# Sinkhorn-sorted attention with top-1 experts: q loaded first, sort operands made earlier

## The chip, the cores and the metric

One NeuronCore of a Trainium2 chip runs the whole program; the other cores are idle. The metric is the device time of one execution in microseconds (us), lower is better. Engine names: PE is TensorE, DVE is VectorE, ACT is ScalarE, POOL is GpSimd, SP is SyncE. PSUM is the memory into which PE writes; the other engines evict results from it to SBUF.

## What is computed

Two stages, one after the other (q, k, v: batch 4, 8 heads, 768 rows, head width 64, float32):

```python
P = sort_net                                   # (4, 8, 8, 8)
for _ in range(5):
    P = np.exp(P - P.max(-1, keepdims=True))
    P = P / (P.sum(-1, keepdims=True) + 1e-09)
    P = P / (P.sum(-2, keepdims=True) + 1e-09)
k_sorted = np.einsum('bhij,bhjcd->bhicd', P, k_b)   # 8 blocks of 96 rows
v_sorted = np.einsum('bhij,bhjcd->bhicd', P, v_b)
attn = softmax(scale * q_b @ k_sorted.T)       # inside each block of 96
x = (attn @ v_sorted), as 3072 rows of 512
e = argmax(x @ w_gate)                         # 8 experts
out = softmax(x @ w_gate)[e] * (relu(x @ w1[e]) @ w2[e])
```

The expert weights are 512 x 1024 and 1024 x 512 for each of 8 experts.

## The kernel before

The work runs batch by batch (four batches of 768 rows). For batch b the kernel guesses one expert from the mean of v (the vote: vote_sum and vote_pick on PE, vote_read on DVE, lines 222 to 245), POOL reads the winner into a register (read_vote) and loads that expert's w1 and w2. All 768 rows of the batch go through that expert; rows of another expert would be done in a loop behind everything (line 704), which is entered only if the count rest_i is over zero.

Order. manual_schedule keeps every engine's instructions in the order in which the code emits them. So the order of the lines is the order in each engine's queue, and an instruction that waits holds all later ones of its engine. All loads of q, k, v and weights are issued by POOL (they convert float32 to bf16 on the way), in one queue; the two small loads and the output go by SP.

Start (lines 129 to 335). POOL issues v, q and k (three parts) of batch 0. PE spins on a zero tile (spin, line 164, one idle matmul of 512 columns each) while nothing is there. Sinkhorn is a loop of five rounds (304 to 325), each an Exp on ACT and six small DVE instructions. In the rounds' gaps stand constants (gap1 to gap4), the vote of batch 0, and the first of three relays: relay (192) copies a part of v on DVE into the tile vr, from which the sort of v reads its weights. expand_k and expand_v are copies of the identity, spread over columns; only batch 0's part is made here, on DVE.

Sort operands. make_pk and make_pv (342, 363) turn Sinkhorn's result snb into block matrices pk and pv: a few matmuls with expand_k or expand_v put snb on the partitions (tile rep in PSUM, tag "f", of which there are three buffers), then DVE multiplies, sums and multiplies again. With pk and pv, sort_k (382, 16 matmuls for 8 of 24 columns) and sort_v (399) sort a batch; turn_q (177) transposes a third of q on PE. Each leaves its PSUM tile to an eviction.

Planner. The object clk (19 to 48) is an estimate, made when the program is built, of when PE, ACT and DVE are free; evac, hidden and outputs ask it (pick) which of ACT and DVE evicts. weave (51) mixes two generators: the attention of batch b as main, with an estimate in us for each yield, and the expert of batch b - 1 as fill, of which it takes pieces in proportion. hidden (504) is one fill step of four matmuls into a PSUM buffer of tag "f" and a Relu; outputs (517) has two steps of four matmuls.

Batch 0 (560 to 603). spin(3), the three turn_q, two q copies on ACT (copy_q), make_pk, spin(4), make_pv, the third q copy, then the sorts with relays and single spins between, then scores, values and turn of each of the eight blocks (steps, 605), from block 5 on woven with the first eight hidden steps.

Batches 1 to 3 (attention, 627 to 671): vote_sum, vote_pick, half of relay, vote_read, loads, route of the batch before (the gate, 467: 24 small matmuls and seven DVE instructions), the other half of relay, two turn_q, sort_v, sort_k, the last turn_q, and steps. In batch 1 alone, the rest of expand_k and expand_v is copied by DVE, make_pv for batches 1 to 3 stands ahead of turn_q and make_pk for them ahead of sort_v.

End (679 to 697). After two fill steps of the last expert comes its route, after eight more the count of the rows whose expert was not the voted one: DVE compares (hit), sums (count, cb), one matmul (tot, 693) adds over the partitions, DVE makes rest_i. The other fill steps follow.

Of the kernel before, what the change touches and what calls it, by code (L numbers as in the profile page):

```python
# [64 lines left out]
def kernel(  # L65
# [65 lines left out]
    wg32 = consts.tile([P, DC, E], F32)  # L131
    nc.sync.dma_start(out=wg32, in_=moe_w_gate.rearrange("(c p) e -> p c e", p=P))
    load_v(0)
    load_qk(q, q_in, "q_in", 0, 1)
    ident = consts.tile([P, P], BF16)
# [113 lines left out]

    def load_w1(ev):  # L250
        t = wpool.tile([P, DC, F], BF16, tag="w1")
        nc.gpsimd.dma_start(out=t, in_=w1_r[bass.ds(ev, 1)].rearrange(  # L252
            "e p c f -> p (e c) f"))
        return t
# [37 lines left out]
    def gap3():  # L292
        nc.vector.reduce_sum(kj, kc.rearrange("p (h j) -> p j h", j=NB), axis=AX.X)
        nc.vector.tensor_copy(expand_v[:, :H], ident[:BH, :H, None].to_broadcast(
            [BH, H, NB * 2]))
# [3 lines left out]
    def gap4():  # L299
        nc.vector.tensor_copy(expand_k[:, :H], ident[:BH, :H, None].to_broadcast(  # L300
            [BH, H, NB * CQ]))
        vote_read(0, lg0)

    for it in range(5):
        nc.scalar.activation(sn, sn, ACT.Exp)
        if it == 1:
            gap1()
            finish_wv()
        elif it == 2:
            gap2()  # L310
        elif it == 3:
            vote_sum(0)
            gap3()
        elif it == 4:
# [11 lines left out]

    ev = read_vote(0)
    w1t = load_w1(ev)
    load_v(1)
    wexp[0] = (w1t, load_w2(ev))  # L330
    note_vote(0)
    load_qk(q, q_in, "q_in", 1, 1)
    load_qk(k, k_in, "k_in", 1, 1)
    nc.gpsimd.memset(vr[1][:, :, HB:, :], 0.0)
    nc.gpsimd.memset(ksT[1][:, :, :, HB:], 0.0)

# [4 lines left out]

    def make_pk(bs):
        n = 2 * len(bs)
        rep = psp.tile([P, n, NB, NB], F32, tag="f", bufs=3)
        for g in range(n):
            h0 = bs[0] * H + g * H2
            nc.tensor.matmul(out=rep[:, g].rearrange("p i j -> p (i j)"),
                             lhsT=expand_k[:, h0:h0 + H2].rearrange("p h x -> p (h x)"),
                             rhs=snf, start=(g == 0), stop=(g == n - 1),
                             skip_group_check=True)  # L350
        sel = small.tile([P, n * NB, NB], F32, tag="sel")
        nc.vector.tensor_mul(sel, rep.rearrange("p g i j -> p (g i) j"),
# [9 lines left out]

    def make_pv(bs):
        n = len(bs)
        rep = psp.tile([P, n, NB, NB], F32, tag="f", bufs=3)
        for g, b in enumerate(bs):
            nc.tensor.matmul(
                out=rep[:, g].rearrange("p i j -> p (i j)"),
                lhsT=expand_v[:, b * H:(b + 1) * H].rearrange("p h x -> p (h x)"),
                rhs=snf, start=(g == 0), stop=(g == n - 1), skip_group_check=True)  # L370
        sel = small.tile([P, n * NB, NB], F32, tag="sel")
        nc.vector.tensor_mul(sel, rep.rearrange("p g i j -> p (g i) j"),
# [186 lines left out]

    spin(3)  # L560
    qps = [turn_q(0, g, ("s", "v", "t")[g]) for g in range(3)]

    def copy_q(engine, g):
        engine(q_dst(0, g), qps[g].rearrange("p c x -> p x c"))

    copy_q(nc.scalar.copy, 0)
    copy_q(nc.scalar.copy, 1)
    make_pk([0])
    spin(4)
    make_pv([0])  # L570
    copy_q(nc.scalar.copy, 2)
    clk.act, clk.dve, clk.pe = 2.0, 1.0, 1.0
    sort_k(0, 0, "s")
    spin(1)
    relay(0, 16, 16)
    sort_k(0, 1, "v")
    spin(1)
    relay(0, 32, 32)
    for g in range(2):
        sort_v(0, 8 * g, 8, "f", 3)  # L580
    sort_k(0, 2, "s")
# [44 lines left out]

    def attention(b):
        vote_sum(b)
        yield 0.6
        lg = vote_pick(b)  # L630
        relay(b, 0, D // 2)
# [14 lines left out]
        yield 0.6  # L646
        if b == 1:
            nc.vector.tensor_copy(expand_k[:, H:], ident[:BH, H:BH, None].to_broadcast(
                [BH, BH - H, NB * CQ]))
            nc.vector.tensor_copy(expand_v[:, H:], ident[:BH, H:BH, None].to_broadcast(  # L650
                [BH, BH - H, NB * 2]))
            make_pv([1, 2, 3])
        piece_q(b, 0, "s")
        piece_q(b, 1, "v")
        yield 1.2
        if b == 1:
            make_pk([1, 2, 3])
        n = D // 4
# [98 lines left out]
```

## Time and profile before

| | |
|---|---|
| device time, median of 3 runs | 180.6 us (180.13 to 181.26) |
| the profiled execution, its own time | 180.92 us |
| its span, first to last instruction | 179.0 us |
| mean granted clock of PE | 0.935 |
| busy, share of the span | PE 86%, DVE 57%, ACT 50%, POOL 13% |
| DMA packets | 24.51 MB, mean 137 GB/s |

The span is what the trace covers; the device time of the same execution has 1.9 us more around it. A busy share is a mean over stages with different limits, so it doesn't say what a change in one stage is worth. The chain that ended last is followed back from the last instruction: at each step to what released it, or to the instruction before it on its engine. In the timeline a row is a run of like instructions: its start, its length, the engine, the line of the code, the operation with tiles and shapes, how many (x), and in brackets how long the engine stood idle before it and what released it. The granted clock is 1.00 at 2.4 GHz and 0.50 at 1.2 GHz.

### The profile page before, as it was taken

The page shows a single profiled execution, that of the slowest core. Times are in us where ns is not written, and L with a number is a line of the kernel's source. Part 1 is how long each engine was busy: PE and PEld are TensorE (multiplying, and loading weights), DVE is VectorE, ACT ScalarE, POOL GpSimd, SP SyncE. Part 2 cuts the span into 40 slices and gives each one's busy share as a digit, 9 for nine tenths or more (in the row PEclk, how much of TensorE's full clock was granted, in tenths as well). Part 3 has the DMA queues.
Part 4 walks back from the last instruction along what each step waited for, and adds up shares of the span by engine and source line. Part 5 has one row for each costly group of instructions (what it writes and reads, how often), then busy time and mean ns, then how long its engine had stood idle before and what let it go on. Part 6 is the DMA issues. An engine that isn't in the chain of part 4 may idle for free.

```text
span 179.0 us, 5141 instructions
## 1 busy us (share of the span) xinstructions
PE 154.5 (86%) x2229; PEld 95.0 (53%) x2244; DVE 102.4 (57%) x249; ACT 89.8 (50%) x146; POOL 23.8 (13%) x47
## 2 busy tenths in 40 slices
PE   7379679989387999999999999899999998969960
PEld 2146566656255555567665555576655555535420
DVE  6964865554894655758565575386655653542220
ACT  3215664535284757627775556276756563523110
POOL 7939000000800000003500000040000000000000
PEclk9957955599999999999999999999999999999997
DMA  4999999920699998211999997219971222000441
GB/s 47 194 207 200 215 202 213 215 48 4 78 195 210 211 212 229 108 62 64 157 200 220 207 226 234 85 40 168 181 123 59 103 76 108 13 0 0 157 146 62
DMA packets 13626, 24.51 MB, mean 137 GB/s; under 512 B 1312, under 2 KB 6176, under 8 KB 13600
## 3 DMA queue, kind: packets, MB, share of 16 engines
q0 software_dynamic: 9568, 17.83, 55.8%
q1 hardware_dynamic: 4032, 6.32, 9.8%
q8 instruction: 19, 0.31, 0.7%
q14 instruction: 7, 0.06, 0.1%
HBM read 35.68 MB, written 6.29 MB: 234 GB/s over the span
## 4 chain that ended last, share of the span: by engine, by line
PE 73%; DVE 13%; DMA 6%; ACT 3%; issue 3%; POOL 0%; DVEq 0%; ACTq 0%; POOLq 0%
PE ps L507 24%; PE ps L520 22%; PE av L438 6%; DMA t<-in_q_dram 6%; PE sc L419 4%; PE t L181 4%; PE t L403 4%; PE tp L457 3%; PE t L387 3%; DVE xo L446 3%; DVE o L538 2%; PE lg L472 1%; ACT xT L175 1%; DVE ksT L173 1%; DVE vr L197 1%
## 5 line engine op out<-in xcount | busy, mean ns | idle before, releaser
L507 PE MATMUL ps<-xT,t 128*128 128x384 bf16 x256 | 49.1, 332 | 0.1
L520 PE MATMUL ps<-t,hT 128*128 128x512 bf16 x179 | 45.4, 379 | 0.8 <-issue 0.2
L428 ACT ACTIVATE ex<-sc 128x768 bf16<-128x768 f32 x32 | 25.9, 809 | 12.3 <-PE sc L419 12.2
L507 PEld LDWEIGHTS <-t 128*128 128x128 bf16 x256 | 22.7, 99 | 14.2 <-issue 0.7
L515 ACT ACTIVATE hT<-ps 128x384 bf16<-128x384 f32 x39 | 19.2, 492 | 20.5 <-PE ps L507 20.5
L520 PEld LDWEIGHTS <-hT 128*128 128x128 bf16 x192 | 16.5, 97 | 15.4
L513 DVE TENSOR_SCALAR hT<-ps 128x384 bf16<-128x384 f32 x25 | 13.9, 557 | 16.5 <-PE ps L507 16.4
L446 DVE TENSOR_TENSOR xo<-av,rec 96x512 bf16<-96x512 f32 x32 | 22.0, 687 | 1.1
L538 DVE TENSOR_SCALAR o<-ps,gw 128x512 f32<-128x512 f32 x11 | 8.3, 750 | 14.5 <-PE ps L520 14.1
L438 PEld LDWEIGHTS <-ex 128*128 128x128 bf16 x256 | 11.7, 103 | 9.0 <-DVE xo L446 3.0
L252 POOL DMA_DIRECT2D t<-in_moe_w_dram x4 | 3.6, 903 | 95.2 <-DVE gw L493 34.0
L438 PE MATMUL av<-vs,ex 128*128 128x65 bf16 x256 | 14.4, 203 | 2.2 <-DVE xo L446 1.5
L175 ACT COPY xT<-tp 128x384 bf16<-128x384 bf16 x20 | 9.6, 478 | 12.6 <-PE tp L457 12.6
L536 ACT ACTIVATE o<-ps,gw 128x512 f32<-128x512 f32 x13 | 8.9, 687 | 13.3 <-PE ps L520 13.2
L444 DVE RECIPROCAL rec<-av 96x8 f32<-96x8 f32 x32 | 6.4, 200 | 15.7 <-PE av L438 15.6
L419 PE MATMUL sc<-qT,ksT 64*128 64x96 bf16 x256 | 12.0, 218 | 1.9 <-DVE ksT L173 1.4
L173 DVE CAST vs<-t 128x1024 bf16<-128x1024 f32 (+1 forms) x10 | 10.0, 1008 | 5.8 <-PE t L403 5.8
L457 PE MATMUL tp<-ident,xo 96*128 96x96 bf16 x128 | 11.6, 216 | 1.4 <-ACT xT L175 1.1
L403 PE MATMUL t<-pv,vr 128*64 128x64 bf16 x512 | 10.9, 200 | 1.3 <-DVE vs L173 1.3
L419 PEld LDWEIGHTS <-ksT 64*128 64x128 bf16 x256 | 7.1, 99 | 9.2 <-issue 5.6
L403 PEld LDWEIGHTS <-vr 128*64 128x64 bf16 x512 | 9.7, 115 | 3.5 <-issue 2.5
L457 PEld LDWEIGHTS <-xo 96*128 96x128 bf16 x128 | 8.4, 103 | 4.8 <-issue 1.3
(94 smaller groups left out, 151.4 us busy)
## 6 DMA issues: line engine op xcount, KB each, us to landing
t<-in_moe_w_dram POOLq DMA_DIRECT2D x8, 1024.0 KB, 11.6
out_dram<-o SPq DMA_DIRECT2D x24, 256.0 KB, 2.0
v_in<-in_v_dram POOLq DMA_DIRECT2D x4, 768.0 KB, 14.5
t<-in_q_dram POOLq DMA_DIRECT2D x4, 768.0 KB, 19.2
t<-in_k_dram POOLq DMA_DIRECT2D x3, 768.0 KB, 22.9
t<-in_k_dram POOLq DMA_DIRECT2D x3, 256.0 KB, 10.4
sn<-in_sort_net_dram SPq DMA_DIRECT2D x1, 8.0 KB, 1.5
wg<-in_moe_w_gate_dram SPq DMA_DIRECT2D x1, 16.0 KB, 1.9
```

Of the source, the lines that this page charges most:

```text
L173: nc.vector.tensor_copy(dst, src)
L403: nc.tensor.matmul(out=t[f * HP:(f + 1) * HP, u, :], lhsT=vr[b % 2][:, (d0 + u) // 2, :, (d0 + u) % 2], rhs=pv[b][:, f * H:(f + 1) * H, :] ...
L419: nc.tensor.matmul(out=sc[:, r, h4 * BLK:(h4 + 1) * BLK], lhsT=ksT[b % 2][rows, x].rearrange("p f c -> p (f c)"), rhs=qT[b % 2][rows, x * ...
L428: nc.scalar.activation(ex[:, :H * BLK].rearrange("p (t c) -> p t c", t=2), sc[:, :, :H2 * BLK], ACT.Exp, scale=scale)
L438: nc.tensor.matmul(out=av4[:, h // 4, h % 4, :], lhsT=ex[:, h * BLK:h * BLK + P], rhs=vs[:, b % 2, h * NB + i, :D + 1], start=(h % 4 == 0) ...
L446: nc.vector.tensor_mul(xo, av4[:BLK, :, :, :D], rec.to_broadcast([BLK, 2, 4, D]))
L457: nc.tensor.transpose(out=tp[:, dc, :], in_=xf[:, dc * P:(dc + 1) * P], identity=ident[:BLK, :BLK])
L507: nc.tensor.matmul(out=ps, lhsT=w1t[:, dc, fc * P:(fc + 1) * P], rhs=xT[:, dc, half * NH:(half + 1) * NH], start=(dc == 0), stop=(dc == DC ...
L513: nc.vector.tensor_scalar_max(hT[:, fc, :], ps, 0.0)
L515: nc.scalar.activation(hT[:, fc, :], ps, ACT.Relu)
L520: nc.tensor.matmul(out=ps, lhsT=hT[:, fc, s * P:(s + 1) * P], rhs=w2t[:, fc, :], start=(fc == 0), stop=(fc == FC - 1))
L538: nc.vector.tensor_scalar_mul(o, ps, gw[:, t:t + 1])
```

## The change

It has three parts.

1. Start. The loads of batch 0 are issued in the order q, v, k. The three turn_q and the three q copies (on ACT) stand inside the Sinkhorn loop, in rounds 3 and 4 (counted from 0); expand_k and expand_v are made whole, for all four batches, by ACT in rounds 0 to 2. The vote and the first relay leave the loop. PE gets spin(6) behind the loop, and the spins of 3, 4, 1 and 1 go. make_pk and make_pv are split: spread_k and spread_v hold the matmuls, make_pk and make_pv the rest. Behind the loop stand both spreads, vote_sum, relay, make_pk, make_pv, vote_pick, relay, vote_read, relay; then the loads, with v of batch 1 ahead of the expert's weights and w1 in two halves of its columns. The sorts of k and v alternate, and clk starts with other times.
2. Batch 1. The spreads for batches 1 to 3 are the first of attention(1), make_pv follows, make_pk stands between vote_sum and vote_pick, with yields of 2.4 us that the time of main is raised by.
3. End. Eight fill steps stand between cb and the matmul tot.

The diff, without the parts of make_pk and make_pv that only split the functions:

```diff
+    load_qk(q, q_in, "q_in", 0, 1)
     load_v(0)
-    load_qk(q, q_in, "q_in", 0, 1)
...
-    def load_w1(ev):
+    def load_w1(ev, parts=1):
         t = wpool.tile([P, DC, F], BF16, tag="w1")
-        nc.gpsimd.dma_start(out=t, in_=w1_r[bass.ds(ev, 1)].rearrange(
-            "e p c f -> p (e c) f"))
+        n = F // parts
+        for i in range(parts):
+            nc.gpsimd.dma_start(
+                out=t[:, :, i * n:(i + 1) * n],
+                in_=w1_r[bass.ds(ev, 1), :, :, i * n:(i + 1) * n].rearrange(
+                    "e p c f -> p (e c) f"))
...
+    def expand(dst, h0, n):
+        shp = [BH, n, dst.shape[-1]]
+        nc.scalar.copy(dst[:, h0:h0 + n], ident[:BH, h0:h0 + n, None].to_broadcast(shp))
+
+    def copy_q(g):
+        nc.scalar.copy(q_dst(0, g), qps[g].rearrange("p c x -> p x c"))
 
     for it in range(5):
         nc.scalar.activation(sn, sn, ACT.Exp)
-        if it == 1:
+        if it == 0:
+            expand(expand_k, 0, 2 * H)
+        elif it == 1:
+            finish_wv()
+            expand(expand_k, 2 * H, 2 * H)
             gap1()
-            finish_wv()
         elif it == 2:
+            expand(expand_v, 0, BH)
             gap2()
         elif it == 3:
-            vote_sum(0)
+            qps = [turn_q(0, g, ("s", "v", "t")[g]) for g in range(3)]
+            copy_q(0)
             gap3()
         elif it == 4:
-            lg0 = vote_pick(0)
-            gap4()
-            relay(0, 0, 16)
+            copy_q(1)
+            copy_q(2)
...
+    spin(6)
...
-    spin(3)
-    qps = [turn_q(0, g, ("s", "v", "t")[g]) for g in range(3)]
...
-    copy_q(nc.scalar.copy, 0)
-    copy_q(nc.scalar.copy, 1)
-    make_pk([0])
-    spin(4)
-    make_pv([0])
-    copy_q(nc.scalar.copy, 2)
-    clk.act, clk.dve, clk.pe = 2.0, 1.0, 1.0
+    rep_k = spread_k([0])
+    rep_v = spread_v([0])
+    vote_sum(0)
+    relay(0, 0, 16)
+    make_pk([0], rep_k)
+    make_pv([0], rep_v)
+    lg0 = vote_pick(0)
+    relay(0, 16, 16)
+    vote_read(0, lg0)
+    relay(0, 32, 32)
+
+    load_v(1)
+    ev = read_vote(0)
+    w1t = load_w1(ev, 2)
+    wexp[0] = (w1t, load_w2(ev))
+    note_vote(0)
+    load_qk(q, q_in, "q_in", 1, 1)
+    load_qk(k, k_in, "k_in", 1, 1)
...
+    clk.act, clk.dve, clk.pe = 13.2, 16.0, 13.6
     sort_k(0, 0, "s")
-    spin(1)
-    relay(0, 16, 16)
+    sort_v(0, 0, 8, "f", 3)
     sort_k(0, 1, "v")
-    spin(1)
-    relay(0, 32, 32)
-    for g in range(2):
-        sort_v(0, 8 * g, 8, "f", 3)
+    sort_v(0, 8, 8, "f", 3)
+    clk.pe = 16.2
     sort_k(0, 2, "s")
...
     def attention(b):
+        if b == 1:
+            rep_v = spread_v([1, 2, 3])
+            rep_k = spread_k([1, 2, 3])
+            yield 0.6
+            make_pv([1, 2, 3], rep_v)
+            yield 0.6
         vote_sum(b)
         yield 0.6
+        if b == 1:
+            make_pk([1, 2, 3], rep_k)
+            yield 1.2
         lg = vote_pick(b)
...
-        if b == 1:
-            nc.vector.tensor_copy(expand_k[:, H:], ident[:BH, H:BH, None].to_broadcast(
-                [BH, BH - H, NB * CQ]))
-            nc.vector.tensor_copy(expand_v[:, H:], ident[:BH, H:BH, None].to_broadcast(
-                [BH, BH - H, NB * 2]))
-            make_pv([1, 2, 3])
...
-        if b == 1:
-            make_pk([1, 2, 3])
...
     nc.vector.tensor_copy(cb, count)
+    for _ in range(FC):
+        next(fill)
     tot = psp.tile([P, 1], F32, tag="t")
```

## Rows read from the trace of the kernel before

**Rows 1.** The page, part 4: shares of the chain by engine.

```profile
PE 73%; DVE 13%; DMA 6%; ACT 3%; issue 3%; POOL 0%; DVEq 0%; ACTq 0%; POOLq 0%
```

**Rows 2.** The chain in order of time, 0 to 62 us: start us, us, what.

```profile
2.13 9.96 DMA t<-in_q_dram
...
12.13 2.77 PE t L181 x48
...
25.04 0.61 PE av L438 x8
...
35.39 1.23 PE ps L507 x4
...
39.22 0.40 PE av L438 x8
...
41.55 0.65 PE ps L507 x4
...
50.73 0.48 DVE sel L352
...
51.82 1.30 DVE pk L358 x6
```

**Rows 3.** The timeline, start of the kernel: start us, us, engine, line, operation [idle before].

```profile
7.95 0.26 ACT L305 ACTIVATE sn<-sn 32x64 f32<-32x64 f32 x1 [1.55 <-DVE sn L325]
...
8.46 0.76 PE L225 MATMUL t<-vmask,v_in 128*128 128x8 bf16 x24 [2.95 <-DMA v_in<-in_v_dram]
...
9.80 0.26 ACT L305 ACTIVATE sn<-sn 32x64 f32<-32x64 f32 x1 [0.38 <-DVE sn L325]
...
11.85 0.77 POOL L252 DMA_DIRECT2D t<-in_moe_w_dram  x1 [2.76 <-DVE red L323]
...
11.86 0.43 DVE L325 TENSOR_TENSOR snb<-sn,red 32x64 bf16<-32x64 f32 x1
...
13.24 2.84 ACT L564 COPY qT<-t 128x1024 bf16<-128x1024 bf16 x3 [3.19 <-PE t L181]
...
14.84 0.28 PE L347 MATMUL rep<-snb,expand_k 32*128 32x64 bf16 x2
...
15.80 0.49 DVE L358 TENSOR_TENSOR pk<-ksel,pt 128x128 bf16<-128x128 f32 x2
...
18.15 1.01 ACT L175 CAST ksT<-t 128x1024 bf16<-128x1024 f32 x1 [2.06 <-PE t L387]
...
21.61 0.34 PE L419 MATMUL sc<-qT,ksT 64*128 64x96 bf16 x8 [1.43 <-DVE ksT L173]
```

**Rows 4.** Line 121, the loads of q and k issued before 9 us.

```profile
L121 POOL DMA_DIRECT2D t<-in_k_dram x3: 721/722/733, 3.5 to 5.0; - x3
...
DMA to landing us min/median/max: 9.9/10.2/11.0
```

**Rows 5.** Table by stretches of 2 us (engines' busy us, granted clock, DMA share, GB/s).

```profile
14.00:16.00 2.00, 1.67 (x22) 1.19 (x20) 0.77 (x3) 2.00 (x3) 1.86 (x5) 0.51 1.12 185
...
16.00:18.00 2.00, 2.00 (x37) 1.16 (x35) 1.55 (x6) 0.09 (x1) 1.72 (x2) 1.00 1.12 212
...
22.00:24.00 2.00, 1.73 (x66) 1.57 (x66) 1.32 (x3) 1.41 (x2) 0.00 (x0) 0.69 1.03 211
...
36.00:38.00 2.00, 2.00 (x28) 1.12 (x26) 0.37 (x2) 1.19 (x2) 0.00 (x0) 0.89 0.45 88
```

**Rows 6.** The same table by stage: the first part of attention, batches 1 and 2.

```profile
41.90:61.40 19.50, 14.79 (x330) 10.30 (x330) 13.90 (x34) 9.78 (x15) 4.32 (x6) 1.00 0.86 148
...
78.90:93.96 15.06, 15.06 (x333) 10.62 (x330) 10.30 (x20) 10.11 (x16) 3.97 (x6) 1.00 0.69 126
```

**Rows 7.** The timeline of batch 1 from its first spread.

```profile
48.11 0.26 PE L367 MATMUL rep<-snb,expand_v 32*128 32x64 bf16 x3 [2.79 <-DVE expand_v L650]
...
49.18 0.69 DVE L378 TENSOR_TENSOR pv<-vh,pt 128x128 bf16<-128x128 f32 x3
```

**Rows 8.** The timeline of the tail at line 693.

```profile
158.67 0.18 PE L693 MATMUL tot<-cb,ones 128*128 128x1 bf16 x1 [1.59 <-DVE cb L691]
```

More of the change, by code (lines that the diff above doesn't have):

```diff
@@ L293, in gap3 @@
         nc.vector.reduce_sum(kj, kc.rearrange("p (h j) -> p j h", j=NB), axis=AX.X)
-        nc.vector.tensor_copy(expand_v[:, :H], ident[:BH, :H, None].to_broadcast(
-            [BH, H, NB * 2]))
         nc.vector.reduce_sum(vj, ident.rearrange("p (h j f) -> p j h f", h=H, j=NB),
                              axis=AX.XY)
[L299 to L302, printed above, removed]
+    def expand(dst, h0, n):
[3 more added lines that the diff above has]
+        nc.scalar.copy(q_dst(0, g), qps[g].rearrange("p c x -> p x c"))
     for it in range(5):
         nc.scalar.activation(sn, sn, ACT.Exp)
-        if it == 1:
+        if it == 0:
[3 more added lines that the diff above has]
+            expand(expand_k, 2 * H, 2 * H)
             gap1()
-            finish_wv()
         elif it == 2:
+            expand(expand_v, 0, BH)
             gap2()
         elif it == 3:
-            vote_sum(0)
+            qps = [turn_q(0, g, ("s", "v", "t")[g]) for g in range(3)]
+            copy_q(0)
             gap3()
         elif it == 4:
-            lg0 = vote_pick(0)
-            gap4()
-            relay(0, 0, 16)
+            copy_q(1)
+            copy_q(2)
         nc.vector.reduce_sum(red[:, :, 0], sn, axis=AX.X)
@@ L325, with spread_k @@
         nc.vector.tensor_mul(dst, snt, red.to_broadcast([BH, NB, NB]))
[L327 to L335, printed above, removed]
+    spin(6)
     pk, pv = {}, [None] * B
     snf = snb.rearrange("p i j -> p (i j)")
-    def make_pk(bs):
+    def spread_k(bs):
         n = 2 * len(bs)
@@ L350, in make_pk @@
                              skip_group_check=True)
+        return rep
+    def make_pk(bs, rep):
+        n = 2 * len(bs)
         sel = small.tile([P, n * NB, NB], F32, tag="sel")
@@ L361, in make_pk, with spread_v @@
             pk[bs[0] + g // 2, g % 2] = t.rearrange("p h i c -> p (h i c)")
-    def make_pv(bs):
+    def spread_v(bs):
         n = len(bs)
@@ L370, in make_pv @@
                 rhs=snf, start=(g == 0), stop=(g == n - 1), skip_group_check=True)
+        return rep
+    def make_pv(bs, rep):
+        n = len(bs)
         sel = small.tile([P, n * NB, NB], F32, tag="sel")
@@ L556 @@
     EXPERT_US = 2 * (HIDDEN_US + SUB * 1.74)
-    spin(3)
-    qps = [turn_q(0, g, ("s", "v", "t")[g]) for g in range(3)]
-    def copy_q(engine, g):
-        engine(q_dst(0, g), qps[g].rearrange("p c x -> p x c"))
-    copy_q(nc.scalar.copy, 0)
-    copy_q(nc.scalar.copy, 1)
-    make_pk([0])
-    spin(4)
-    make_pv([0])
-    copy_q(nc.scalar.copy, 2)
-    clk.act, clk.dve, clk.pe = 2.0, 1.0, 1.0
+    rep_k = spread_k([0])
[15 more added lines that the diff above has]
+    load_qk(k, k_in, "k_in", 1, 1)
+    nc.gpsimd.memset(vr[1][:, :, HB:, :], 0.0)
+    nc.gpsimd.memset(ksT[1][:, :, :, HB:], 0.0)
+    clk.act, clk.dve, clk.pe = 13.2, 16.0, 13.6
     sort_k(0, 0, "s")
-    spin(1)
-    relay(0, 16, 16)
+    sort_v(0, 0, 8, "f", 3)
     sort_k(0, 1, "v")
-    spin(1)
-    relay(0, 32, 32)
-    for g in range(2):
-        sort_v(0, 8 * g, 8, "f", 3)
+    sort_v(0, 8, 8, "f", 3)
+    clk.pe = 16.2
     sort_k(0, 2, "s")
@@ L674 @@
     for b in range(1, B):
-        weave(attention(b), ATTN_US, fill, EXPERT_US - (HIDDEN_US if b == 1 else 0.0))
+        weave(attention(b), ATTN_US + (2.4 if b == 1 else 0.0), fill, EXPERT_US - (HIDDEN_US if b == 1 else 0.0))
         for _ in fill:
```

## The prediction

> **What bounds the kernel now.** The page's chain by engine first: of the work that ended last, 73% is TensorE (PE), 13% VectorE (DVE), 6% DMA [rows 1]. So a us counts where PE stands still, or where another engine or a load carries the chain. The chain in order of time tells where that is [rows 2]: until 12.1 us everything hangs on q's load, then come 2.77 us of q's transposes, then Sinkhorn's result is spread and pk and pv are made, and at last PE stands idle before the first scores at 21.61, for 1.43 us, until DVE has evicted ksT; the timeline of the start shows that wait [rows 3]. In the table by stage, the attention of batch 1 takes 19.50 us for 14.79 us of PE work, that of batch 2 15.06 us without a gap [rows 6]. At the end there is one single wait of 1.59 us [rows 8]. TensorE's clock is half (granted 0.51 in 14 to 16 us, 1.2 GHz) when the transposes run, full (2.4 GHz) from 16, half again between some 22.8 and 36.4 us (worked out from the means 0.69 and 0.89 of two stretches), then full [rows 5].
>
> The trace is of an execution of 180.92 us: span 179.0 and 1.9 around it. The median of the runs is 180.6, 0.3 less; the sum is made against 180.92 and 0.3 is taken off at the end.
>
> **Start: q first.** On POOL's DMA queue q's issue goes past v's: it takes v's place at some 1.4 us, where before it stood at 2.13 [rows 2]. v, first before, was usable at 8.46 us [rows 3], q at 12.13, 9.96 us after its issue [rows 2]; both are of the same size. I let q take v's place: 8.5 us, and v q's: 12.1. k's three parts stay third, 9.9 to 11.0 us after their issue at 3.5 to 5.0 [rows 4], so at 13.4, 14.5 and 16.0. The 48 transposes then run from 8.5 to 11.3 at the old 2.77 us.
>
> PE has spin(6) next, idle matmuls of 512 columns. From four matmuls of 384 columns, 1.23 us at half and 0.65 at full clock [rows 2], one of 512 is 0.41 or 0.22 us; six are 2.5 or 1.3 us, so the spreads start between 12.6 and 13.8 (an estimate from these rows). Taken: 13.3, since the clock rose in the trace of before after some 3.9 us of work: PE's began at 12.1 [rows 2], and the clock was full from 16 [rows 5]. The removed spins (3, 4, 1, 1) stood partly in front of the spreads and sorts and pay for this.
>
> Is Sinkhorn done by 13.3? One round is 1.85 us (Exp at 7.95 and 9.80) and the result came at 12.29 [rows 3]. The three expand copies go from DVE to ACT, 512 elements each; ACT copies 1024 in 0.95 to 1.01 us [rows 3], so 0.5 to 0.6 us each. Behind them in ACT's queue waits the next Exp, which DVE waits for: two delays of some 0.4 us. The fifth Exp also waits behind the first q copy: 16 transposes end at 9.4, the copy at 10.4. Then a round of 1.85: 12.3, as before; vote_read and the first relay have left the round, and the delays of Exp have come in. 1 us of slack to the spreads; if q lands 1 us late that is used up, and each further us costs a us.
>
> From the spread to the last pk was 14.84 to 16.29, 1.45 us [rows 3]; now 13.3 to 14.8. vote_sum, 24 small matmuls, lies on PE in that time, the last two q copies on ACT before it. Then the first sort_k (0.6 us on PE) is in PSUM at 15.4; its k part landed at 13.4. The planner's starting clocks (ACT 13.2, DVE 16.0, PE 13.6) give the evictions k0, v0, k1, k2 to ACT: by its arithmetic DVE is dearer each time; DVE has pk, pv, three relays and vote_read until about 17.2. On ACT that is 3 x 1.01 [rows 3], about 0.6 for v0 with half the elements, and 0.1 of gaps: 15.4 to 19.1, and the first scores at 19.2. Before: 21.61. The gain is 2.4; I take 2.3. Bounds: 0.6 (q a us and more later, spins at half, or k's third part late) and 2.9 (DVE takes one eviction more).
>
> Moved past each other on POOL: load_v(1) is issued before the vote is read, the read of the vote waits for vote_read at about 16.3 (before 10.3), and w1 is issued 1.5 us behind it as before (11.85, [rows 3]): 17.9. Behind that wait on POOL stand w1's two halves, w2, batch 1's q and k and two memsets. The DMA engines have k until 16.0 and v of batch 1 until 19.8 at the 212 GB/s of [rows 5], so the wait leaves them no gap to speak of; w1 (1.05 MB) lands at 25 to 26, w2 five us later, q and k by 39. The first hidden block runs some 2 us before the one at 35.39 [rows 2], now at 31; 5 us of cover. If that cover went, each us late would cost a us.
>
> **The clock, unknown.** The half-speed stretch began after PE had stood idle for 1.43 us before the scores at 21.61 [rows 3, 5]. That idle time shrinks to about 0.5 us, so the stretch may come later, be shorter or not come. What it is worth: a step's values are 0.61 us at half and 0.40 at full clock [rows 2], five steps make 1.0; hidden blocks 1.23 against 0.65, two of them 1.2; together 2.2. Bounds: minus 1.0 (it starts as early and ends at the same time as now, with two more hidden blocks in it) and plus 2.2. Taken: plus 1.0, between the ends, because the idle time in front of it is the only thing the rows show ahead of its start.
>
> The Trainium skill has a rule against this place: transposes on TensorE don't count as work for the clock ("TensorE: Matmul & The Clock Gate", Part 4: PE-mode transpose). By it the 2.77 us of transposes would not help the clock up, and it would rise late. Here it rose at 16 us, after work from 12.1 of which 2.77 us were transposes [rows 2, 5]; so the trace speaks against it, without excluding it. It is the third rival.
>
> **Batch 1.** The expand copies of batches 1 to 3 are gone from here, made by ACT at the start. make_pv (from the spread at 48.11 to 49.87, its own work 1.4 us [rows 7]) and make_pk (50.73 to 53.12, 2.4 us [rows 2]) move in front of the vote, and their spreads in front of everything. Before, PE waited 2.79 us for expand_v [rows 7], because route, both relays and the copies stood ahead of it on DVE. Walked by hand with row durations from the spreads at 0: make_pv ends at 2.1; the second hidden block waits for no one; make_pk's first multiply stands on DVE behind an eviction and ends at 3.6, until when the third hidden block lacks a PSUM buffer (two of three hold the spreads): PE waits 1.2 us. make_pk ends at 5.4, relay 6.8, vote_read 7.2: q's second transposes wait 0.9 us for that PSUM bank. Later 0.5. The sorts end, with all nine hidden blocks, at 16.2 to 17, against 19.3 before (from 42.0 to 61.3, within the stage of [rows 6]). Gain 2.4, bounds 0.3 (each moved wait as long as the old) and 4.4 (as dense as batch 2). The walk decides for the middle. The later w1 issue of batch 1 has 30 us of cover.
>
> **End.** The matmul tot moves eight fill steps back. Its wait of 1.59 us [rows 8] goes: the hit counting on DVE ends long before. Nothing else waits for rest_i until the kernel's end. Gain 1.5, bounds 1.3 and 1.6: after it PE runs the same matmuls without a gap to the end.
>
> **Sum.** 2.3 + 1.0 + 2.4 + 1.5 = 7.2; 180.92 - 7.2 - 0.3 = 173.4 us.
>
> **Rivals.**
> First: in batch 1 the wait only moves, from expand_v to the PSUM buffers and the vote behind make_pk. For it: DVE is busy 13.90 us in this stage against 10.30 in batch 2's [rows 6], and 1.4 and 2.4 us of the difference stay, in order and in front of relay and route. Against it: these stand beside hidden blocks and vote matmuls now. Gain there 0.3: 175.5.
> Second: the start is bound by what lands anyway. k's third part comes at 16.0 in either kernel [rows 4], and sort_k's evictions follow. If q shares the engines with v and lands late, or k lands later, the start gains 0.6: 175.1.
> Third: the clock rises only behind the sorts. Spins and first sort at half: 16 transposes at half are 0.92 us of the 2.77 [rows 2], against 0.5 at full; spins 0.5 us more, sort_k 0.5 more, and the 1.0 of the clock term not gained: 175.4. The Trainium skill's rule on transposes (above) would do this.
> Fourth, slower: with the spins of the sort stage gone and PE waiting for DVE in batch 1, the clock stays at half through the first expert. Place: 31 to 56 us. Price: 16 hidden blocks at half in place of two, 14 x 0.58 = 8.1 us, and the 1.0 not gained: 182.5. It decides from some 11 more hidden blocks at half (6.4 us) on. Against it: the wait of 2.79 us at 48 us left the clock at 1.00 [rows 6], and dense hidden blocks brought it back at 36.4.
> That the change does not do what it says is part of the first two.
>
> **How the numbers follow.** Forecast 0.60, own range 171.5 to 175; first 0.14, second 0.10, third 0.10, fourth 0.03; the rest, 0.03, is two of the first three together: 177 to 179. A measurement of this kernel tells about 1%, 1.8 us, from no change: under 178.8 is faster, over 182.4 slower. Faster: 0.60 + 0.14 + 0.10 + 0.10 less 0.02 of tails: 0.92; within 1%: 0.05; slower: 0.03. Range 170.3 (all upper bounds of start, half of the rest) to 177.3 (first and second together).
>
> **What would show it.** Right: the first transpose at 8.5, the first scores at 19 to 20, batch 1's stage at 16 to 17.5 us, no PE wait at tot, and the half-speed stretch shorter than 13.6 us. Wrong: L419 of batch 0 after 20.5 (start); a PE wait of 2 us and more on a PSUM buffer or on the vote in batch 1; granted clock 0.50 beyond 36 us; PE waiting for w1.

## The result

The changed kernel takes 172.59 us (median of 4 runs, 171.98 to 174.27), the kernel before beside it 180.93 us; the ratio is 0.954, 95% interval 0.9437 to 0.9644. Forecast were 173.4 us, 170.3 to 177.3. The mean granted clock of one kernel differs from run to run (before: 0.915 to 0.972 over seven runs on one chip, which took 178.05 to 183.16 us; changed: 0.943 to 0.988 over eight), so the ratios here are taken over those runs of each kernel that lie within 1.5% of its fastest, and parts of 1 or 2 us are read below from stretches of a trace between two marks on PE.

The profiled execution took 171.98 us, its span is 170.1. It is the fastest of the four. The ledger, in us, from the timelines of the two profiled executions; the last column is another execution of the changed kernel (174.32 us, span 172.4), which was taken later, as the run "the changed kernel again":

| stretch | before | changed | gain | forecast | changed again |
|---|---|---|---|---|---|
| start to the first scores | 21.61 | 18.54 | 3.07 | 2.3 | 19.95 |
| to the first PE work of batch 1 | 20.43 (at 42.04) | 18.22 (at 36.76) | 2.21 | 1.0 (clock) | 17.35 |
| to vote_sum of batch 2 | 36.71 (at 78.75) | 34.69 (at 71.45) | 2.02 | 2.4 | 36.34 |
| to the route of batch 3 | 72.36 | 72.37 | 0 | 0 | 72.38 |
| to the start of the last eviction | 22.06 | 20.29 | 1.77 | 1.5 | 20.28 |
| to the end of the span | 5.83 | 5.99 | -0.16 | 0 | 6.10 |

The first three rows differ between the two executions of the changed kernel by 1.4, 0.9 and 1.7 us, because the clock fell at other places and because PE's stop of 1.04 us at 20.07 (last section) is in the first alone; so each gain there holds for the executions that it was read from.

The page of the changed kernel, parts 2 and 4, beside [rows 1]:

```profile
PEclk9959999999999999999999999999999999999999
...
PE 75%; DVE 9%; ACT 5%; DMA 4%; issue 3%; POOLq 0%
```

DVE's share of the chain has gone from 13% to 9%, DMA's from 6% to 4%, and but for one stretch the clock is full. The start in the timeline, which answers to [rows 3]:

```profile
8.47 2.40 PE L181 MATMUL t<-ident,t 128*64 128x128 bf16 x48 [2.96 <-DMA t<-in_q_dram]
...
11.20 1.81 PE L167 MATMUL t<-idle 128*128 128x512 bf16 x5 [0.33 <-issue]
...
11.62 0.43 DVE L333 TENSOR_TENSOR snb<-sn,red 32x64 bf16<-32x64 f32 x1
...
12.94 0.23 PE L348 MATMUL rep<-snb,expand_k 32*128 32x64 bf16 x2
...
13.85 0.49 DVE L363 TENSOR_TENSOR pk<-ksel,pt 128x128 bf16<-128x128 f32 x2
...
15.10 1.01 ACT L175 CAST ksT<-t 128x1024 bf16<-128x1024 f32 x1 [1.02 <-PE t L396]
...
16.56 1.93 ACT L175 CAST ksT<-t 128x1024 bf16<-128x1024 f32 x2
...
17.34 1.48 POOL L254 DMA_DIRECT2D t<-in_moe_w_dram  x2 [7.75 <-DVE vr L197]
...
18.54 0.34 PE L428 MATMUL sc<-qT,ksT 64*128 64x96 bf16 x8 [0.81 <-ACT ksT L175]
```

q is there at 8.47 (v was at 8.46), Sinkhorn's result at 12.05, the spreads start at 12.94 behind the spins, pk is ready at 14.34. From 15.10 to 18.49 ACT evicts k0, v0, k1, k2 without a gap of note, and PE waits 0.81 us for the last of them: ACT is the bound of the start in this execution. Batch 1, which answers to [rows 7], and the end, to [rows 8]:

```profile
36.76 0.26 PE L372 MATMUL rep<-snb,expand_v 32*128 32x64 bf16 x3
...
44.13 0.64 PE L181 MATMUL t<-ident,t 128*64 128x128 bf16 x16 [1.92 <-DVE eid L244]
...
46.03 0.70 PE L412 MATMUL t<-pv,vr 128*64 128x64 bf16 x32 [0.51 <-ACT qT L175]
```

```profile
155.25 0.17 PE L711 MATMUL tot<-cb,ones 128*128 128x1 bf16 x1
```

The spread waits for nothing now. In its place q's second transposes wait 1.92 us for vote_read, which stands behind make_pk on DVE, and the first sort of v 0.51 us. At tot there is no wait.

### The profile page after: what moved, and what is told of

It reads as the page before. It is cut to its first block, busy times and chain, and to the rows that moved or that the text cites. A ratio compares the mean times of both kernels' runs of the same rounds, so it can differ in the third digit from the quotient of the medians.

```text
span 170.1 us, 5137 instructions
## 1 busy us (share of the span) xinstructions
PE 148.1 (87%) x2226; PEld 91.2 (54%) x2241; DVE 101.1 (59%) x247; ACT 90.5 (53%) x147; POOL 24.7 (15%) x48
## 4 chain that ended last, share of the span: by engine, by line
PE 75%; DVE 9%; ACT 5%; DMA 4%; issue 3%; POOLq 0%
PE ps L516 24%; PE ps L529 23%; PE av L447 6%; PE t L412 4%; DMA t<-in_q_dram 4%; PE sc L428 4%; PE t L181 4%; PE t L396 3%; PE tp L466 3%; DVE xo L455 3%; ACT ksT L175 2%; ACT qT L175 2%; PE t L225 1%; DVE o L547 1%; DVE hT L522 1%
## 5 line engine op out<-in xcount | busy, mean ns | idle before, releaser
L516 PE MATMUL ps<-xT,t 128*128 128x384 bf16 x256 | 47.7, 326 | 0.6 <-ACT xT L175 0.3
L524 ACT ACTIVATE hT<-ps 128x384 bf16<-128x384 f32 x36 | 17.7, 491 | 14.6 <-PE ps L516 14.6
L522 DVE TENSOR_SCALAR hT<-ps 128x384 bf16<-128x384 f32 x28 | 15.6, 556 | 12.0 <-PE ps L516 11.7
L254 POOL DMA_DIRECT2D t<-in_moe_w_dram x5 | 4.4, 889 | 86.2 <-PE t L181 30.1
L447 PE MATMUL av<-vs,ex 128*128 128x65 bf16 x256 | 13.1, 194 | 2.9 <-DVE xo L455 2.1
L447 PEld LDWEIGHTS <-ex 128*128 128x128 bf16 x256 | 10.4, 97 | 9.5 <-DVE xo L455 3.9
L173 DVE CAST vs<-t 128x1024 bf16<-128x1024 f32 (+1 forms) x11 | 10.6, 980 | 7.0 <-PE t L412 6.9
L428 PE MATMUL sc<-qT,ksT 64*128 64x96 bf16 x256 | 11.0, 205 | 1.4 <-ACT ksT L175 0.8
L181 PE MATMUL t<-ident,t 128*64 128x128 bf16 x192 | 7.7, 236 | 4.9 <-DMA t<-in_q_dram 3.0
L466 PE MATMUL tp<-ident,xo 96*128 96x96 bf16 x128 | 10.7, 205 | 1.3 <-ACT xT L175 1.1
```

The costliest lines, as they stand in the source:

```text
L181: nc.tensor.transpose(out=t[r * D:(r + 1) * D, u, :], in_=q_in[b][:, r, g * 8 + u, :], identity=ident)
L428: nc.tensor.matmul(out=sc[:, r, h4 * BLK:(h4 + 1) * BLK], lhsT=ksT[b % 2][rows, x].rearrange("p f c -> p (f c)"), rhs=qT[b % 2][rows, x * ...
L447: nc.tensor.matmul(out=av4[:, h // 4, h % 4, :], lhsT=ex[:, h * BLK:h * BLK + P], rhs=vs[:, b % 2, h * NB + i, :D + 1], start=(h % 4 == 0) ...
L466: nc.tensor.transpose(out=tp[:, dc, :], in_=xf[:, dc * P:(dc + 1) * P], identity=ident[:BLK, :BLK])
L516: nc.tensor.matmul(out=ps, lhsT=w1t[:, dc, fc * P:(fc + 1) * P], rhs=xT[:, dc, half * NH:(half + 1) * NH], start=(dc == 0), stop=(dc == DC ...
L522: nc.vector.tensor_scalar_max(hT[:, fc, :], ps, 0.0)
```

## The experiments

The theory after the result was the prediction's, with the ledger's sizes: start bound by q and then by evictions, the clock kept up by the shorter idle time before the scores, batch 1 gained by the order of make_pv and make_pk, the end by the wait at tot. The rivals: the gain of batch 1 belongs to the expand copies alone; the clock does not hang on that idle time; load order, spins and w1's place decide nothing.

**The end alone.** The kernel before, with

```diff
+    for _ in range(FC):
+        next(fill)
     tot = psp.tile([P, 1], F32, tag="t")
```

> The kernel before with the third part alone: eight fill steps between cb and the matmul tot. Theory: the part is worth the wait of 1.59 us that PE had there, and perhaps 0.2 more, since the trace of the changed kernel is 1.77 us shorter from route of batch 3 to the last eviction: 1.6 to 1.8 us less than before, with no PE wait at tot. Rival: the evictions of the hidden blocks queued on DVE behind the counting already cost that time elsewhere, so that the wait only moves: 0 to 0.5 us.

The time alone shows nothing: 181.32 us, median of 10 runs, against 179.94 (13 runs), the granted clock of eight of its runs being 0.91 to 0.94. The stretch does: from the route of batch 3 to the start of the last eviction its trace has 153.37 to 173.66, 20.29 us, as the changed kernel, against 22.06. So it is 1.77 us in this execution, at the place that the theory names.

**Batch 1's order undone.** The changed kernel, without the 2.4 us that weave got for batch 1, and with

```diff
-        if b == 1:
-            rep_v = spread_v([1, 2, 3])
-            rep_k = spread_k([1, 2, 3])
-            yield 0.6
-            make_pv([1, 2, 3], rep_v)
-            yield 0.6
...
-        if b == 1:
-            make_pk([1, 2, 3], rep_k)
-            yield 1.2
...
+        if b == 1:
+            make_pv([1, 2, 3], spread_v([1, 2, 3]))
         piece_q(b, 0, "s")
         piece_q(b, 1, "v")
         yield 1.2
+        if b == 1:
+            make_pk([1, 2, 3], spread_k([1, 2, 3]))
```

> The changed kernel with batch 1's operands made where the kernel before makes them (spread_v and make_pv ahead of turn_q, spread_k and make_pk ahead of the sorts), the expand copies still made by ACT at the start. Theory: the order of make_pv and make_pk is what gained 2.0 us in batch 1's stage, so 1.3 to 2.0 us more than the changed kernel (0.7 us belong to the expand copies, which stay gone). Rival: the order gave nothing, only the absent expand copies did: within 0.5 us of the changed kernel, since the new order pays 1.92 us of PE wait for the vote behind make_pk.

173.31 us (4 runs, 172.34 to 174.25), ratio to before 0.9655 (0.957 to 0.974). The rival holds. Its timeline of batch 1:

```profile
37.16 0.74 PE L225 MATMUL t<-vmask,v_in 128*128 128x8 bf16 x24
...
40.37 0.26 PE L372 MATMUL rep<-snb,expand_v 32*128 32x64 bf16 x3
...
43.62 1.20 PE L412 MATMUL t<-pv,vr 128*64 128x64 bf16 x64 [0.94 <-DVE pv L387]
...
47.92 0.70 PE L412 MATMUL t<-pv,vr 128*64 128x64 bf16 x32 [1.71 <-DVE vs L173]
```

vote_sum of batch 2 comes at 71.74: 34.58 us for the stretch, against 34.69 in the new order and 36.71 before. The spread at 40.37 waits for nothing although it stands where it stood. Two other waits, 0.94 for pv and 1.71 for an eviction of v behind make_pk, take the place of the new order's 1.92 and 0.51. So the order is worth nothing; what the copies themselves are worth is the next run's question.

**The copies alone.** The kernel before, with the change's three copies on ACT in Sinkhorn's rounds 0 to 2 and

```diff
-            nc.vector.tensor_copy(expand_k[:, H:], ident[:BH, H:BH, None].to_broadcast(
-                [BH, BH - H, NB * CQ]))
-            nc.vector.tensor_copy(expand_v[:, H:], ident[:BH, H:BH, None].to_broadcast(
-                [BH, BH - H, NB * 2]))
```

> The kernel before with one piece of the change: expand_k and expand_v made whole by ACT inside Sinkhorn, no expand copies by DVE anywhere; all else in the old order. Theory, after the run that undid batch 1's order: these copies alone are what batch 1 lost. PE's transposes of q stood behind spread_v, which waited 2.79 us for a copy at the end of DVE's queue; without it the stretch from vote_sum of batch 1 to that of batch 2 falls from 36.7 to 34.6 us as it did there; the start gets 0 to 0.5 us later, since Exp waits behind the copies on ACT. In all 1.6 to 2.2 us less than before. Rival: the wait moves on to pv, and the stretch keeps 36 us or more.

180.24 us (4 runs) against 181.41 (13 runs, 176.97 to 183.97), ratio 1.0135 (0.9985 to 1.0286): the 1.6 to 2.2 us that were expected do not show in the time. Its first scores come at 23.15, 1.54 later than before; 1.09 of that is q, which landed at 13.22 in place of 12.13. The stretch is 41.36 to 77.48, 36.12 us, only 0.6 less than before. Its PE timeline says why; below it stands the kernel before's row that answers to the one at 52.09:

```profile
44.57 0.26 PE L371 MATMUL rep<-snb,expand_v 32*128 32x64 bf16 x3
...
47.79 1.20 PE L407 MATMUL t<-pv,vr 128*64 128x64 bf16 x64 [0.92 <-DVE pv L382]
...
52.09 1.01 PE L407 MATMUL t<-pv,vr 128*64 128x64 bf16 x32 [1.71 <-DVE vs L173]
...
53.04 2.73 PE L511 MATMUL ps<-xT,t 128*128 128x384 bf16 x8
```

```profile
54.31 0.69 PE L403 MATMUL t<-pv,vr 128*64 128x64 bf16 x32 [1.26 <-DVE vs L173]
```

The wait for expand_v is gone, the two waits of the run above are there (0.92 and 1.71), and behind the second the clock has fallen: eight matmuls of hidden take 2.73 us here, 1.47 in the run above, and the row ahead of it 1.01 in place of 0.70. Without these 1.57 us the stretch would be 34.55 (an estimate from these rows). From vote_sum to that row are 10.73 us here and 10.76 in the run above, against 12.27 before: the copies are worth 1.5 us up to there, in both runs. The other 0.6 of the 2.1 us (36.71 against 34.58) lies behind the row; 0.39 of it is a stop in the kernel before, at 57.36, for which the profile names no cause and which is in neither run. This execution gave 1.6 us back through the clock: the prediction's rival, the wait that moves on, in another form.

**The idle time before the scores filled.** The kernel before, with

```diff
     sort_v(0, 24, 8, "f", 3)
+    spin(6, "t", 1)
```

> The kernel before with one addition: six idle matmuls on PE between the last sort ahead of the first scores and these scores, where PE stood idle for 1.43 us. They take about 1.3 us, so they hold up nothing. Theory: that idle time is what let the clock fall at 22.8 us; with it filled, the granted clock stays at 1.00 and the stretch to the first matmuls of batch 1 (20.4 us from the scores) is 2.2 us shorter: about 178.5. Rival: the clock falls anyway, because of the steps behind the scores: within 0.5 us of before.

177.93 us (4 runs, 176.65 to 180.3) against 179.94, ratio 0.9871 (0.9789 to 0.9952). In its trace:

```profile
22.61 0.34 PE L419 MATMUL sc<-qT,ksT 64*128 64x96 bf16 x8
...
32.19 0.50 PE L419 MATMUL sc<-qT,ksT 64*128 64x96 bf16 x8
...
41.02 0.74 PE L225 MATMUL t<-vmask,v_in 128*128 128x8 bf16 x24
```

The wait of 1.43 us before the scores is gone, and scores take 0.34 us, full clock, in the first six steps; before, they took 0.50 from the second on. The clock fell once all the same, near 31.4 us. From the scores to vote_sum of batch 1 are 18.41 us, against 20.43 before and 18.22 in the changed kernel, 2.0 less, as the theory has it. But the times overlap (before: 177.36 to 184.29), and the trace of the run with the copies alone speaks against that reading: its start is the old one, with the wait unfilled.

```profile
23.15 0.34 PE L423 MATMUL sc<-qT,ksT 64*128 64x96 bf16 x8 [1.42 <-DVE ksT L173]
...
30.43 0.50 PE L423 MATMUL sc<-qT,ksT 64*128 64x96 bf16 x8
...
31.99 0.34 PE L423 MATMUL sc<-qT,ksT 64*128 64x96 bf16 x8
...
41.36 0.74 PE L225 MATMUL t<-vmask,v_in 128*128 128x8 bf16 x24
```

From the scores to vote_sum of batch 1 are 18.21 us there, as short as with the wait filled. The clock fell there too, at 24.9 us, but it was full again at 31.7, ahead of the first hidden block; in the kernel before only at 36.4, behind two of them. In the run of the end alone, with 1.28 us of the same wait, it fell at 24.6 and rose at 38.1: 20.72 us. So in all three executions with the wait the clock fell 1 to 2.5 us behind the first scores, and with the wait filled some 9 us behind them: that the idle time brings the fall on fits these four. What the fall costs hangs on when the clock rises again, and by that the three differ by 2.5 us; what decides it no run shows, so the 2.0 us are not shown to be the price of the idle time.

**No spins behind Sinkhorn.** The changed kernel without spin(6).

> The changed kernel without its six idle matmuls behind Sinkhorn. The spreads can start 0.8 us earlier (Sinkhorn's result is there at 12.05, the spreads began at 12.94). Theory: the transposes raise the clock as other matmuls do, but without the spins PE stands idle from 10.9 to 12.1 and the clock rises later, at 16 us or after; the sorts run at half, the scores come at 18.3 to 19, and the clock may stay at half into the steps: 0 to 2 us more than the changed kernel. Rival one: the transposes alone suffice, the clock rises at about the same time, and the kernel is 0.3 to 0.8 us shorter. Rival two, as the Trainium skill has it, that transposes don't count as work for the clock: then it does not rise before the sorts have run, as in the theory, but also with the spins it would not have risen at 12.2 us.

172.39 us (4 runs, 172.08 to 172.93), ratio 0.9591 (0.952 to 0.9661): the same time as with them.

```profile
8.54 2.77 PE L181 MATMUL t<-ident,t 128*64 128x128 bf16 x48 [3.03 <-DMA t<-in_q_dram]
12.55 0.26 PE L347 MATMUL rep<-snb,expand_k 32*128 32x64 bf16 x2 [1.25 <-DVE snb L333]
...
14.16 1.06 PE L395 MATMUL t<-pk,t 128*64 128x128 bf16 x16
...
18.98 0.50 PE L427 MATMUL sc<-qT,ksT 64*128 64x96 bf16 x8 [0.25 <-ACT ksT L175]
...
20.68 0.34 PE L427 MATMUL sc<-qT,ksT 64*128 64x96 bf16 x8
```

The 16 matmuls of sort_k take 1.06 us and the scores at 18.98 take 0.50, so the clock came up only behind the sorts, as the theory had it; still the scores are 0.44 us later only, because ACT's evictions are the bound, and the spreads begin 0.4 earlier. So the full clock that the spins bought in the changed kernel's trace brought it 0.44 us at the scores; and they don't always keep it: with the order undone, and in the changed kernel again, the clock fell in the middle of the sorts, and the scores came at 20.01 and 19.95. What the transposes do for the clock, the second rival, is taken up in the last section.

**v first.** The changed kernel with load_v(0) ahead of load_qk of q.

> The changed kernel with the first loads in the old order, v then q. Theory: q lands at 12.1 us in place of 8.4; the fifth Exp of Sinkhorn stands behind the first q copy on ACT, so Sinkhorn's result comes 3 us later (about 15), and with it spreads, pk and the first scores: 21.3 to 22, some 3 us later than in the changed kernel, 175 to 176 in all. Rival: the load order is worth little, since k lands last in either kernel and the sorts wait for it; then the scores come within 1 us of 18.5.

176.52 us (10 runs, 175.52 to 178.42), 3.9 more than the first four runs of the changed kernel and 2.6 more than its runs on the same chip (below).

```profile
13.06 1.01 ACT L306 COPY qT<-t 128x1024 bf16<-128x1024 bf16 x1 [4.55 <-PE t L181]
13.97 0.25 ACT L309 ACTIVATE sn<-sn 32x64 f32<-32x64 f32 x1
...
16.94 0.23 PE L348 MATMUL rep<-snb,expand_k 32*128 32x64 bf16 x2
...
19.89 1.06 PE L396 MATMUL t<-pk,t 128*64 128x128 bf16 x16 [0.33 <-DVE eid L244]
...
23.34 0.34 PE L428 MATMUL sc<-qT,ksT 64*128 64x96 bf16 x8 [0.25 <-ACT ksT L175]
```

ACT waits for q's first transposes until 13.06, and the fifth Exp, ready long before, runs at 13.97 behind the copy (10.11 in the changed kernel). The spreads come at 16.94, 4.0 us later, the scores at 23.34, 4.8 us later and even 1.7 later than before: the theory, and dearer than it said. The last 0.8 goes with the clock: the second and third sort_k ran at half (1.06 us at 19.89, 0.64 in the changed kernel). So q's copies inside Sinkhorn need the new load order; the new load order with the copies where they stood before was not run.

**w1 first and whole.** The changed kernel, with

```diff
-    load_v(1)
     ev = read_vote(0)
-    w1t = load_w1(ev, 2)
+    w1t = load_w1(ev)
+    load_v(1)
```

> The changed kernel with w1 in one piece and issued ahead of v of batch 1, as in the kernel before. Theory: both are cover only; the DMA queue runs dry between k's end at 16 us and w1's issue at 17.3 and is then some 2 us behind, but nobody waits for it: the same time within 0.5 us. Rival: the loads become late, v of batch 1 or its q and k, and batch 1 waits: 1 us or more.

173.04 us (4 runs, 172.37 to 174.41): the same. The table by 2 us shows the queue dry:

```profile
16.00:18.00 2.00, 1.85 (x80) 1.74 (x79) 1.76 (x4) 2.00 (x4) 0.44 (x1) 1.00 0.00 0
```

DMA moves 0 GB/s in 16 to 18 us, and no one waits for it; vote_sum of batch 2 stands at 71.51 against 71.45. The order of v and w1 and w1's halves are cover only.

**Late blocks.** The changed kernel, with make_pv and make_pk cut in two (the blocks of batch 1 at once, those of batches 2 and 3 from a list called behind the sorts), without the 2.4 us in weave, and in attention

```diff
+        late = []
         if b == 1:
-            rep_v = spread_v([1, 2, 3])
-            rep_k = spread_k([1, 2, 3])
-            yield 0.6
-            make_pv([1, 2, 3], rep_v)
-            yield 0.6
+            late.append(make_pv([1, 2, 3], spread_v([1, 2, 3])))
         vote_sum(b)
...
+        if b == 1:
+            late.append(make_pk([1, 2, 3], spread_k([1, 2, 3])))
         n = D // 4
...
         piece_q(b, 2, "v")
         yield 2.0
+        for f in late:
+            f()
```

> An attempt at a faster one. The changed kernel, but in batch 1 only spread_v and the first third of make_pv stand ahead of vote_sum, spread_k and the first third of make_pk ahead of the sorts as in the kernel before, and the blocks of batches 2 and 3 (two multiplies for pv, four for pk, 1.3 us of DVE) behind the sorts. Theory: what held PE in batch 1 in both orders is DVE's queue: the vote behind make_pk (1.92 us) in the one, pv (0.94) and an eviction behind make_pk (1.71) in the other. With the blocks moved, PE waits 0.5 to 1 us in all, and the stretch from vote_sum to vote_sum falls from 34.6 to 33 or 33.5: 1 us less than the changed kernel. Rival: the wait comes back at the steps, where the late blocks hold up rec and xo: no gain.

170.62 us (4 runs, 169.26 to 171.26): below all eight runs of the changed kernel.

```profile
35.69 0.26 PE L375 MATMUL rep<-snb,expand_v 32*128 32x64 bf16 x3
...
44.30 0.70 PE L419 MATMUL t<-pv,vr 128*64 128x64 bf16 x32 [0.46 <-DVE vs L173]
...
47.71 0.58 PE L403 MATMUL t<-pk,t 128*64 128x128 bf16 x14 [0.68 <-issue]
...
51.65 0.89 DVE L364 TENSOR_TENSOR pk<-ksel,pt 128x128 bf16<-128x128 f32 x4
```

One wait of 0.46 us for DVE is left, 0.68 at 47.71 that the profile names no cause for, and the late blocks at 51.65 hold up nothing. From the first spread (35.69) to vote_sum of batch 2 (68.80) are 33.11 us against 34.69: 1.6 less. The theory holds; the next two kernels have the late blocks too, and 33.33 and 33.19 us there.

**The changed kernel again, k1 on DVE, four spins.** Three runs on one chip. The second is the kernel of late blocks, with

```diff
-        lg = psp.tile([P, E], F32, tag="v")
+        lg = psp.tile([P, E], F32, tag="t" if b == 0 else "v")
...
-    relay(0, 32, 32)
...
+    clk.act, clk.dve, clk.pe = 13.2, 15.0, 13.6
     sort_k(0, 0, "s")
+    sort_k(0, 1, "v")
+    relay(0, 32, 32)
+    clk.run_dve(0.8, 0.0)
     sort_v(0, 0, 8, "f", 3)
-    sort_k(0, 1, "v")
-    sort_v(0, 8, 8, "f", 3)
-    clk.pe = 16.2
+    clk.pe = 15.6
     sort_k(0, 2, "s")
+    sort_v(0, 8, 8, "f", 3)
```

and the third is this with spin(4) for spin(6).

> The changed kernel once more, beside the next two on the same chip. Expected as at first: 172 to 174 us, first scores at 18.5 us, 34.7 us from the first spread of batch 1 to vote_sum of batch 2; where the wait of 1.9 us for the vote lets the clock fall, 0.8 more.

> The kernel with late blocks, and in the start the second sort_k right behind the first, evicted by DVE in place of ACT, with the third relay behind it (the vote's PSUM tile moves to another bank so that this sort does not wait for vote_read). Theory: what sets the first scores is ACT's row of four evictions (k0, v0, k1, k2: 15.1 to 18.5); with k1 on DVE beside them the scores come 0.5 us earlier, at 17.8 to 18.0, and all is 0.5 us shorter than with late blocks (170.6). Rival: PE or k's landing is the bound, the scores stay within 0.2 of 18.4; or the relay, now later, holds up the sorts of v behind the scores and gives it back.

> The same with four idle matmuls in place of six behind Sinkhorn. Theory: the spreads wait for the spins (12.9, Sinkhorn's result is there at 12.05), so up to 0.5 us comes off the start, if the clock is up when the sorts begin; if it rises only behind them, the sorts run at half and the gain is gone, as in the kernel without spins: 0.5 less to 0.3 more than with six.

Medians of 4 runs: 173.9 (173.4 to 176.18), 172.19 (170.93 to 174.59), 171.07 (170.6 to 172.28); ratios to the same runs of before 0.9695 (0.9614 to 0.9776), 0.9585 (0.9489 to 0.9681), 0.9557 (0.948 to 0.9634). In the first, the changed kernel again:

```profile
16.61 0.96 PE L396 MATMUL t<-pk,t 128*64 128x128 bf16 x16 [0.33 <-DVE eid L244]
...
19.95 0.43 PE L428 MATMUL sc<-qT,ksT 64*128 64x96 bf16 x8 [0.25 <-ACT ksT L175]
...
44.66 1.06 PE L181 MATMUL t<-ident,t 128*64 128x128 bf16 x16 [1.92 <-DVE eid L244]
```

Two of its expectations failed. The clock fell at 16.8 us, in the middle of the sorts, so the scores came at 19.95 and not at 18.5; and in the wait of 1.92 us it fell again and was at half from 44 to 50.8, so the stretch from the first spread to vote_sum of batch 2 took 36.34 us, 1.65 more than 34.69 and not 0.8. In the second:

```profile
14.79 1.01 ACT L175 CAST ksT<-t 128x1024 bf16<-128x1024 f32 x1 [1.02 <-PE t L403]
...
15.43 1.22 DVE L173 CAST ksT<-t 128x1024 bf16<-128x1024 f32 x1
...
16.02 0.64 PE L403 MATMUL t<-pk,t 128*64 128x128 bf16 x16 [0.38 <-DMA t<-in_k_dram]
...
17.77 0.34 PE L435 MATMUL sc<-qT,ksT 64*128 64x96 bf16 x8 [0.34 <-ACT ksT L175]
...
20.01 0.67 PE L419 MATMUL t<-pv,vr 128*64 128x64 bf16 x30 [1.70 <-issue]
...
22.07 0.51 PE L435 MATMUL sc<-qT,ksT 64*128 64x96 bf16 x8 [0.40 <-ACT ex L444]
```

DVE evicts k1 beside ACT, and the scores come at 17.77, 0.8 us earlier than in the changed kernel: the eviction row was the bound. k's third part, 0.38 us of wait, is next. But a wait of 1.70 us at 20.01 follows, with a half clock behind it (scores 0.51 us), and takes the gain back in this execution; the third relay, which the rival had in suspicion, had ended at 17.44. With four spins the scores come at 18.11 and that wait is 0.43; what four instead of six bring was not told apart, since the spreads came at 13.14, later than with six (12.62). The third is the fastest measured beside the changed kernel on one chip: its four runs lie below all four of that one.

## Why the prediction was right, and where it was not

The time and its direction came out. The sum was 1.7 us short of the first execution (7.2 against 8.9 of span) and 0.6 above the second (6.6), which split the gain otherwise; that the two totals lie on either side of the forecast is in part luck, since the clock, which decides the split, was not foreseen in either. One of the four reasons was wrong. The lower end of the range, 170.3, does not follow from its words: all of the start's upper bound and half of the rest's room give some 9.4 us, 171.2.

Start: right in each link, mis-sized by 0.8 in the first execution and by 0.6 the other way in the second (1.66). q landed as v had; Sinkhorn ended at 12.05 (said 12.3), the spreads began at 12.94 (13.3), and ACT's four evictions took 15.10 to 18.49 (15.4 to 19.1). 3.07 us is above the upper bound of 2.9. The run with v first shows that the order of the loads carries it, the run with k1 on DVE that the evictions bound it while the clock is full; with the sorts at half, in the second execution, PE waits only 0.25 us for ACT. The 3.9 us of work from which 13.3 was taken left out what PE had done from 8.46 on [rows 3].

The clock: the step taken at plus 1.0 between its ends measured 2.2, the whole of the upper end, but this is the sum of two things. In the three runs that run these steps in this order at full clock and without a stop in the sorts (w1 first, late blocks, v first), the stretch takes 17.25, 17.31 and 17.26 us: against the kernel before the half clock cost some 3.1, more than the upper bound, and the changed kernel's stop of 1.04 us at 20.07, which no one foresaw, took some 0.9 back. That the sum met the bound is luck. The idle time was named as the cause with one argument; it fits where the clock fell, but the run with the copies alone shows the same short stretch with the wait in place, so why the half-speed stretch was so long in the kernel before stays open. The third rival came in half: in the first execution all three sort_k ran at full clock, but in the second, and in the run of the order undone, the second and third ran at half. The fourth did not come; but the second execution has its sign, a granted clock of 0.50 behind 36 us (from 44 to 50.8).

Batch 1: 2.0 in place of 2.4, but by another road. The step that failed is the walk from which "the order" took its 2.4 us. It held up a hidden block by 1.2 us for a PSUM buffer, which did not happen (0.29), and q's transposes by 0.9, which was 1.92, just under the 2 us that the prediction had named as a sign of being wrong; above all it counted what the new order's waits would cost, and not what the old order would cost without the copies. That order costs the same (34.58 against 34.69). The first rival, that the wait only moves, was right for the order and wrong for the copies, whose absence gives 1.5 us or more of the 2.0; in the second execution the clock took all but 0.4 back.

End: right, 1.77 for 1.5. The wait was 1.59, and the run with this part alone has the same 1.77, as has the second execution. The other 0.18 is the end of the last matmul ahead of the wait, which lies under the next one where a row goes on: 56 matmuls of hidden, from 144.43 to 153.53, are 0.163 us each, so the 32 ahead of the wait would have been 5.20 us, and the trace of before has 5.36.

Cover: w1 was issued at 17.34 (said 17.9), nobody waited, and its order could be taken back at no price.

## What to carry to other kernels

An instruction that waits at the head of a strictly ordered queue costs everything behind it: look at what the waiting one waits for, and make a constant early on an engine that has time, before moving work around it; then test the order and the constant apart. Where the clock falls after idle time, a wait costs its length and then the half-speed stretch behind it, so that the same stretch of the same kernel took 34.69 us in one execution and 36.34 in another, with the same wait of 1.92 us; such edits are judged by stretches between marks, at like clock, and in more than one execution. When a bound goes, ask which evictions stand in one row on one engine next.

## What was not expected of the hardware

PE stood still in the middle of a row of matmuls for a cause that the profile does not name ("issue"): 1.04 us in the changed kernel, 1.70 with k1 on DVE.

```profile
18.81 0.22 PE L412 MATMUL t<-pv,vr 128*64 128x64 bf16 x2
...
20.07 0.66 PE L412 MATMUL t<-pv,vr 128*64 128x64 bf16 x30 [1.04 <-issue]
```

In both, and with four spins (0.43 us), one packet of each of the two queues of kind "instruction" falls into 17 to 19 us, among the loads' packets, which take 88% to 104% of the DMA engines' time there. With w1 first these packets fall into 14 to 17 us, where the loads take 57%, and there is no such wait. They alone don't make it: in the changed kernel again and with the order undone they lie in 17 to 19 us among loads too, and this row of sorts, begun at 20.31 and 20.28, runs without a stop, while the stops of the three end at 20.07, 20.01 and 19.28. A fetch of instructions that queues behind loads, and holds up a PE that comes too early, would look so; no run took it apart, and it stays open.

The Trainium skill says that transposes do not count as work for the clock ("TensorE: Matmul & The Clock Gate", Part 4: PE-mode transpose). This is the run with k1 on DVE:

```profile
8.51 2.77 PE L181 MATMUL t<-ident,t 128*64 128x128 bf16 x48 [3.40 <-DMA t<-in_q_dram]
11.45 1.24 PE L167 MATMUL t<-idle 128*128 128x512 bf16 x5 [0.17 <-issue]
```

The granted clock is half from 7.9 to 11.2 us, and all that PE did in that time is these transposes. The idle matmuls behind them run at full speed: five take 1.24 us, where three of the kernel before, at 9.71, took 1.44. So the clock rose behind nothing but transposes, which speaks against the rule, in one execution. Transposes with 1.25 us of idle time behind them (no spins) did not bring it up in time.

The granted clock of the page and the durations can disagree: in the run without spins the table by stretches says 1.00 from 0 to 40 us, while sort_k's sixteen matmuls take 1.06 us, against 0.64 at full clock. There the durations tell the clock.
